# One attention pair loop, three edits: the row-sum scaling goes to ScalarE, the value load to the front of a pair, the value parts of the last pair ahead of its output splits

## The chip, the core and the metric

The kernel runs on one core of one Trainium2 chip. The metric is the device time of one execution in microseconds (us), the median of several runs. TensorE does matmuls, VectorE, ScalarE and GpSimd the elementwise work, SyncE issues most DMA transfers. In the rows the engines are called PE, DVE, ACT, POOL and SP. A difference of under 0.2% can't be told from none for this kernel.

## What is computed

```python
q_bits = (einsum('bhsd,dk->bhsk', q, proj) > 0)          # and k_bits: 6 bits each
mask = q_bucket[:, :, :, None] == k_bucket[:, :, None, :]
scores = where(mask, scale * q @ k.T, -1e9)
attn = exp(scores - max(scores)); attn = attn / (sum(attn) + 1e-9)
x = (attn @ v) reshaped to (B*S, H*D)
x = (sigmoid(x @ w_gate) * (x @ w_val)) @ w_out           # first MLP
out = g(x @ w_in) @ w_out2                                # second MLP, g piecewise
```

There are 2 batches, 8 heads, 768 positions and a head dimension of 64. The MLPs have 1536 rows and a width of 512. 

## The kernel before

The attention takes two heads at a time: eight pairs, numbered 0 to 7 here, of 12 units each (6 blocks of 128 queries for each of two heads). A unit is scored on TensorE (`sc`, line 301), VectorE takes the row maximum (line 309), ScalarE the exponential with the row sums as a by-product (`P` and `st[:, 1]`, line 313). Then TensorE transposes P (`pt`, line 333), ScalarE writes a half-precision high part (line 342) and VectorE the low part (line 345), and TensorE multiplies with the values (`O`, line 384).

Four units share a tile `st` of row sums. Once all four are there, line 316 on VectorE adds 1e-9 and multiplies with the scale of the values, line 319 takes the reciprocal, GpSimd spreads it (`rb`, line 534), TensorE transposes it (`r`, line 516), ScalarE copies it out (`rs`, line 520), and VectorE scales the output with it (`xr`, line 391). That is done three times a pair.

The values of a pair are scaled by a power of two. VectorE takes their largest magnitude (line 353), a DMA lays it out in one row (`vrow<-vm`), VectorE finds the power, and a second DMA brings it back to 128 partitions (`vm<-vrow`, line 362). Then GpSimd makes three things of the values: the scaled `vr` (line 365), the high part `vh` (line 368) and the low part `vl` (line 372).

The order of all this is written out by hand: a table AT gives each step a time in units (a pair is 12 units), `at(...)` collects the steps, and they are issued sorted by it. Each engine then runs its instructions in just that order, and an instruction that waits holds up all behind it on its engine.

In the last pair GpSimd also splits the finished outputs of batch 0 for the MLP that follows (`split_x`, lines 538 and 539: `x_0h`, `x_0l`, and so on). After the attention comes the MLP, which is all TensorE.

Of the kernel before, what the change touches and what calls it, by code (L numbers as in the profile page):

```python
# [7 lines left out]
F32 = mybir.dt.float32  # L8
# [5 lines left out]
AF = mybir.ActivationFunctionType  # L14
ALU = mybir.AluOpType
# [12 lines left out]
def lsh_attention_glu_act(ctx, tc, qt, kt, v, proj, w_gate, w_val, w_out1, w_in2, w_out2, ident_d, code_d, out):  # L28
    nc = tc.nc
# [5 lines left out]
    GI = 2  # L35
# [125 lines left out]
    with ExitStack() as actx:  # L161
        ap = actx.enter_context(tc.tile_pool(name="attn", bufs=2))
        pA = actx.enter_context(tc.tile_pool(name="psA", bufs=2, space=PSUM))
        DMA = nc.gpsimd
        NAT, PR = {}, {}
# [120 lines left out]
        class Unit:  # L286
# [26 lines left out]
                nc.scalar.activation(out=self.P, in_=self.sc[:, :, 0:HN], func=AF.Exp, bias=self.st[:, 0, self.c:self.c + 1], scale=1.0, accum_out=self.st[:, 1, self.c:self.c + 1])  # L313

            def ST1(self):
                nc.vector.tensor_scalar(out=self.st[:, 2], in0=self.st[:, 1], scalar1=1e-9, scalar2=VS[self.b, self.p][1], op0=ALU.add, op1=ALU.mult)

            def ST2(self):
                nc.vector.reciprocal(out=self.st[:, 3], in_=self.st[:, 2])
# [27 lines left out]
        def split_v(b, p, h):  # L347
            vr = VR[b, p]
            if h == 0:
                vm = ap.tile([128, 2], F32, tag="vm", name=f"vm_{b}_{p}")  # L350
                row = ap.tile([1, 260], F32, tag="vrow", name=f"vrow_{b}_{p}")
                VS[b, p] = [row, vm]
                nc.vector.tensor_reduce(out=vm[:, 0:1], in_=vr, op=ALU.max, axis=AX.XY, apply_absolute_value=True)
                nc.sync.dma_start(row[:, 0:128], vm[:, 0:1])
            elif h == 1:
                row, vm = VS[b, p]
                u = row.bitcast(U32)
                nc.vector.tensor_reduce(out=row[:, 128:129], in_=row[:, 0:128], op=ALU.max, axis=AX.X)
                nc.vector.tensor_scalar(out=row[:, 129:130], in0=row[:, 128:129], scalar1=VMIN, scalar2=None, op0=ALU.max)
                nc.vector.tensor_scalar(out=u[:, 130:131], in0=u[:, 129:130], scalar1=0x7F800000, scalar2=None, op0=ALU.bitwise_and)  # L360
                nc.vector.tensor_scalar(out=u[:, 132:260], in0=u[:, 130:131].broadcast_to([1, 128]), scalar1=-1.0, scalar2=268.0 * 2.0 ** 23, op0=ALU.mult, op1=ALU.add)
                nc.sync.dma_start(vm[:, 1:2], row[:, 132:260])
                VS[b, p][1] = vm[:, 1:2]
            elif h == 2:
                nc.gpsimd.tensor_scalar(out=vr, in0=vr, scalar1=VS[b, p][1], scalar2=None, op0=ALU.mult)
            elif h == 3:
                vh = ap.tile([128, 2, NI * D], F16, tag="vh", name=f"vh_{b}_{p}")
                nc.gpsimd.tensor_copy(out=vh, in_=vr)  # L368
                VS[b, p].append(vh)
            else:  # L370
                vl = ap.tile([128, 2, NI * D], F16, tag="vl", name=f"vl_{b}_{p}")
                nc.gpsimd.tensor_tensor(out=vl, in0=vr, in1=VS[b, p][2], op=ALU.subtract)
                VS[b, p].append(vl)
# [13 lines left out]
        def evac(b, p, g, O_ps):  # L387
            cs = slice(g * GN, (g + 1) * GN)
            if g == 0:
                X[b, p] = htile(f"xr_{b}_{p}")  # L390
            nc.vector.scalar_tensor_tensor(out=X[b, p][:, cs], in0=O_ps[:, 0:GN], scalar=1.0 / PSCALE, in1=RS.pop((b, p, g)), op0=ALU.mult, op1=ALU.mult)

        NAT, PR, VR, VS, RS, PT, STS = {}, {}, {}, {}, {}, {}, {}
        NU = B * NP * 2 * NI
        PCS = 3
        un = [Unit(n) for n in range(NU)]
# [1 line left out]
        seq = [(b, p) for b in range(B) for p in range(NP)]  # L398
        UP = 2 * NI

        with tc.manual_schedule():
# [98 lines left out]
            def at(kind, i, q, fn, *args):  # L500
                prog.append((UP * q + (AT[kind][i] if isinstance(kind, str) else kind), len(prog), fn, args))

            PP, NQ = {1: p1}, len(seq)
# [22 lines left out]
                w.O = next(w.pv)  # L526

            def SUM(w):
                w.ST1()
                w.ST2()  # L530

            def RB(w):
# [16 lines left out]
            for q in range(NQ):  # L549
                us = un[UP * q:UP * q + UP]  # L550
                for i, w in enumerate(us):
                    at("QK", i, q, w.QK)
                    at("MAX", i, q, w.MAX)
                    at("EXP", i, q, w.EXP)
                for i in range(PCS * NI):
                    x = fl[NI * q + i // PCS]
                    at("T", i, q, x.T, i % PCS)
                    at("HI", i, q, x.HI, i % PCS)
                    at("LO", i, q, x.LO, i % PCS)
                for i in range(NI // GI):  # L560
                    w = us[2 * GI * i + 2 * GI - 1]
                    at("ST", i, q, SUM, w)
                    at("RB", i, q, RB, w)
                    at("R", i, q, R, w)
                    at("RS", i, q, RSC, w)
                    for s in range(3):
                        at("PV", 3 * i + s, q, PV, w, s)
                    at("EV", i, q, lambda w: evac(*w.O), w)
                b, p = seq[q]
                vs = [AT["VR"][0] - UP, AT["VT"][0] - UP, AT["V2"][0], AT["V3"][0], AT["V4"][0]]  # L570
                if q == 0:
                    vs[:2] = AT["MAX"][1] + 0.001, AT["MAX"][2] + 0.3
                    vs[2] = max(vs[2], vs[1] + 0.5)
                    vs[3] = max(vs[3], vs[2] + 0.1)
                    vs[4] = max(vs[4], vs[3] + 0.1)
                for h, d in enumerate(vs):
                    at(d, 0, q, split_v, b, p, h)
                if q + 1 < NQ:
                    at(5.9, 0, q, load_v, *seq[q + 1])
                    if q:  # L580
                        at(min(AT["SCL"][0], AT["TOP"][0], AT["TOP"][1]) - 0.01, 0, q, prep, q + 1)
                        at("SCL", 0, q, on, q + 1, "scale")
                        for j in range(2):
                            at("TOP", j, q, on, q + 1, "top", j)
                            at("RST", j, q, on, q + 1, "rest", j)
                    for i in range(4):
                        at("Z", i, q, on, q + 1, "z", 3 * i, 3 * i + 3)
                        at("XP", i, q, on, q + 1, "xp", *divmod(i, 2))
                        at("H", i, q, on, q + 1, "H", *divmod(i, 2))
                    at("BITS", 0, q, on, q + 1, "bits")  # L590
                    at(AT["TOP"][0] + 0.001 if q else -0.9, 0, q, on, q + 1, "copy", 0, 0)
                    at(AT["TOP"][1] + 0.001 if q else -0.65, 0, q, on, q + 1, "copy", 1, 0)
                    for j in range(2):
                        for m in range(1, 3):
                            at(AT["Z"][3] + 0.01 * m + 0.001 * j, 0, q, on, q + 1, "copy", j, m)
                        for m in range(3, 5):
                            at(AT["H"][2 * j + 1] + 0.01 * m, 0, q, on, q + 1, "copy", j, m)
                    at(max(AT["H"][3], AT["Z"][3]) + 0.06, 0, q, on, q + 1, "done")
                if q + 2 < NQ:
                    at(0.9, 0, q, load_qk, *seq[q + 2])  # L600
            for i in range(10):
                at(2.0 * i, 0, 1, next, fw, None)
            last = NQ - 1
            for c in range(KC):
                at(5.0 + 1.7 * c, 0, last, split_x, 0, c)
            for c in range(KC - 1):
                at(AT["ST"][2] + 0.1 + 0.01 * c, 0, last, split_x, 1, c)
            at(AT["T"][17] + 0.5, 0, last, gv, 0)
# [173 lines left out]
```

## Time and profile before

| what | value |
|---|---|
| median of 3 runs | 839.19 us (838.26 to 839.45) |
| the profiled execution's own time | 836.99 us |
| its span, first to last instruction | 835.2 us |
| TensorE busy | 808.9 us (97%) |
| VectorE busy | 559.4 us (67%) |
| ScalarE busy | 454.0 us (54%) |
| GpSimd busy | 119.6 us (14%) |

The shares are means over two stages. The attention lies in about the first 265 us, where TensorE, VectorE and ScalarE are all busy most of the time; the MLPs fill the rest. A busy TensorE is not one at its peak, since matmuls overlap and their ends are modelled.

### The profile page before, as it was taken

The numbers are of one execution on the slowest core, as the hardware profiler recorded it, in microseconds if no ns is written. First come the engines' busy times: TensorE is split into PE (matmuls) and PEld (weight loads), VectorE is DVE, ScalarE is ACT, GpSimd is POOL, SyncE is SP. The second block draws the span as 40 slices with busy tenths as digits, with TensorE's granted clock in tenths as the row PEclk, the third lists the DMA queues.
The fourth block names the chain that finished last, engine by engine and source line by source line (L and its number), as shares of the span: only waits on it lengthen the run. The fifth ranks groups of instructions, "written<-read, shape, count | busy, mean of one in ns | idle before, by whom it ended". The sixth has DMA issues, their size and how long they took to land.

```text
span 835.2 us, 13047 instructions
## 1 busy us (share of the span) xinstructions
PE 808.9 (97%) x5098; PEld 738.6 (88%) x5098; DVE 559.4 (67%) x979; ACT 454.0 (54%) x869; POOL 119.6 (14%) x104
## 2 busy tenths in 40 slices
PE   7898999999979999999999999999999999999997
PEld 4787888788758999999999999999989898989896
DVE  5899999999963735434588776999943435343443
ACT  3787887888753423222333445547654545455553
POOL 5525623642174000000000000000000000000000
PEclk8999999999999999999999999999999999999999
DMA  8444434443200521221145330543300001000001
GB/s 229 126 106 110 113 95 118 96 123 67 59 1 1 180 74 51 78 74 51 51 148 188 114 107 1 170 152 118 116 1 1 1 1 75 2 1 1 1 0 77
DMA packets 39709, 64.21 MB, mean 77 GB/s; under 512 B 5316, under 2 KB 28228, under 8 KB 39648
## 3 DMA queue, kind: packets, MB, share of 16 engines
q1 hardware_dynamic: 39168, 63.07, 25.9%
q8 instruction: 40, 0.66, 0.3%
q10 hardware_dynamic: 432, 0.20, 0.1%
q14 instruction: 21, 0.17, 0.1%
q0 software_dynamic: 48, 0.11, 0.0%
HBM read 45.27 MB, written 3.15 MB: 58 GB/s over the span
## 4 chain that ended last, share of the span: by engine, by line
PE 81%; DVE 7%; ACT 6%; DMA 3%; POOL 1%; issue 1%; SPq 0%; ACTq 0%; POOLq 0%; DVEq 0%
PE p L126 5%; PE p L128 5%; PE p L127 5%; PE o L688 5%; PE o L689 5%; PE o L687 5%; PE sc L301 5%; PE pt L333 4%; PE pg L128 4%; PE pg L126 4%; PE pv L126 4%; PE pv L127 4%; PE pv L128 4%; PE pg L127 4%; PE y L127 4%; PE y L126 4%
## 5 line engine op out<-in xcount | busy, mean ns | idle before, releaser
L345 DVE SCALAR_TENSOR_TENSOR PT<-pt,PT 128x512 f16<-128x512 f32 x144 | 95.3, 683 | 19.4 <-ACT PT L342 17.1
L342 ACT ACTIVATE PT<-pt 128x512 f16<-128x512 f32 x144 | 82.2, 597 | 34.9 <-PE pt L333 34.8
L313 ACT ACTIVATE P<-sc,st 128x768 f32<-128x768 f32 x96 | 86.8, 904 | 19.1 <-DVE st L309 18.5
L309 DVE TENSOR_REDUCE st<-sc 128x1 f32<-128x768 f32 x96 | 91.0, 948 | 3.1 <-PE sc L301 2.3
L333 PE MATMUL pt<-ident,P 128*128 128x128 f32 x576 | 80.9, 277 | 5.6 <-DVE PT L345 4.9
L126 PE MATMUL p<-yh,wh_i 128*128 128x384 f32 x256 | 86.0, 336 | 0.1
L128 PE MATMUL p<-yh,wl_i 128*128 128x384 f32 x256 | 86.0, 336 | 0.0
L127 PE MATMUL p<-yl,wh_i 128*128 128x384 f32 x256 | 85.8, 335 | 0.0
L333 PEld LDWEIGHTS pt<-ident,P 128*128 128x128 f32 x576 | 67.3, 141 | 15.2 <-DVE PT L345 9.4
L689 PE MATMUL o<-wh_o,gl 128*128 128x512 f32 x192 | 75.4, 393 | 0.0
L688 PE MATMUL o<-wl_o,gh 128*128 128x512 f32 x192 | 75.3, 392 | 0.0
L687 PE MATMUL o<-wh_o,gh 128*128 128x512 f32 x192 | 74.7, 389 | 0.0
L671 DVE SCALAR_TENSOR_TENSOR g<-p,t 128x384 f32<-128x384 f32 x64 | 35.5, 555 | 48.3 <-ACT t L669 48.3
L154 DVE SCALAR_TENSOR_TENSOR h<-sg,pv 128x384 f32<-128x384 f32 x48 | 26.4, 551 | 50.5 <-PE pv L128 50.5
L150 ACT ACTIVATE sg<-pg 128x384 f32<-128x384 f32 x48 | 23.3, 486 | 63.9 <-PE pg L128 61.9
L384 PE MATMUL O<-PT,vh 128*64 128x256 f16 x576 | 55.3, 279 | 1.9 <-POOL vh L368 1.3
L673 DVE TENSOR_TENSOR gl<-g,gh 128x384 fp32r<-128x384 f32 x64 | 35.7, 557 | 31.5 <-ACT gh L672 31.5
L672 ACT ACTIVATE gh<-g 128x384 fp32r<-128x384 f32 x64 | 33.6, 525 | 42.5 <-DVE g L671 42.3
L668 ACT ACTIVATE t<-p,cst 128x384 f32<-128x384 f32 x64 | 36.7, 573 | 36.8 <-PE p L128 36.8
L126 PEld LDWEIGHTS p<-yh,wh_i 128*128 128x128 f32 x256 | 48.1, 188 | 1.5 <-DVE yl L644 0.4
L127 PEld LDWEIGHTS p<-yl,wh_i 128*128 128x128 f32 x256 | 48.1, 188 | 1.1
L116 DVE TENSOR_TENSOR wl_o<-w_o,wh_o 128x512 fp32r<-128x512 f32 x56 | 38.6, 689 | 15.0 <-ACT wh_o L115 15.0
(264 smaller groups left out, 2032.2 us busy)
## 6 DMA issues: line engine op xcount, KB each, us to landing
wr_o<-in_moe_w_out_dram SPq DMA_DIRECT2D x28, 512.0 KB, 3.5
wr_i<-in_moe_w_in_dram SPq DMA_DIRECT2D x16, 512.0 KB, 3.7
wr_g<-in_moe_w_gate_dram SPq DMA_DIRECT2D x12, 512.0 KB, 3.5
wr_v<-in_moe_w_val_dram SPq DMA_DIRECT2D x12, 512.0 KB, 3.9
n<-in_qt_dram SPq DMA_DIRECT2D x8, 384.0 KB, 3.5
n<-in_kt_dram SPq DMA_DIRECT2D x8, 384.0 KB, 3.8
U<-W SPq DMA_DIRECT2D x16, 192.0 KB, 2.6
vr<-in_v_dram SPq DMA_DIRECT2D x8, 384.0 KB, 3.5
```

The source lines that it names most:

```text
L126: nc.tensor.matmul(ps, lhsT=wh, rhs=rh, start=first, stop=False)
L127: nc.tensor.matmul(ps, lhsT=wh, rhs=rl, start=False, stop=False)
L128: nc.tensor.matmul(ps, lhsT=wl, rhs=rh, start=False, stop=last)
L309: nc.vector.tensor_reduce(out=self.st[:, 0, self.c:self.c + 1], in_=self.sc[:, :, 0:HN], op=ALU.max, axis=AX.XY, negate=True)
L313: nc.scalar.activation(out=self.P, in_=self.sc[:, :, 0:HN], func=AF.Exp, bias=self.st[:, 0, self.c:self.c + 1], scale=1.0, accum_out=self. ...
L333: nc.tensor.transpose(self.ps[m][:, j, :], un[2 * self.n + e].P[:, a, c:c + 128], ident)
L342: nc.scalar.activation(out=self.part(0, m), in_=self.ps[m], func=AF.Copy, scale=PSCALE)
L345: nc.vector.scalar_tensor_tensor(out=self.part(1, m), in0=self.ps[m], scalar=PSCALE, in1=self.part(0, m), op0=ALU.mult, op1=ALU.subtract)
L384: nc.tensor.matmul(O_ps[r, 0:GN], lhsT=vv[m][:, e, i * D:(i + 1) * D], rhs=PT[:, l, e * NI + i, :], start=(s == 0), stop=(s == len(steps) ...
L687: nc.tensor.matmul(oacc[i], lhsT=gh[:, ts], rhs=wh, start=(fc == 0), stop=False)
L688: nc.tensor.matmul(oacc[i], lhsT=gh[:, ts], rhs=wl, start=False, stop=False)
L689: nc.tensor.matmul(oacc[i], lhsT=gl[:, ts], rhs=wh, start=False, stop=(fc == F2 - 1))
```

## The change

Line 316 leaves VectorE. In its place ScalarE does `sum * scale + 1e-9 * scale` in one activation, issued right behind the fourth exponential of a group; the product `1e-9 * scale` is made once a pair by a further activation of one element per partition. The reciprocal stays on VectorE where it was. The load of the next pair's values is issued at time 0.8 of a pair instead of 5.9. In the last pair the three value parts are issued on GpSimd from time 1.5 on (6.89 before), and the output splits from 2.2 on, 1.5 apart (from 5.0 on, 1.7 apart).

```diff
             def ST1(self):
-                nc.vector.tensor_scalar(out=self.st[:, 2], in0=self.st[:, 1], scalar1=1e-9, scalar2=VS[self.b, self.p][1], op0=ALU.add, op1=ALU.mult)
+                vm = VM[self.b, self.p]
+                if self.i // GI == 0:
+                    nc.scalar.activation(out=vm[:, 2:3], in_=vm[:, 1:2], func=AF.Copy, scale=1e-9)
+                nc.scalar.activation(out=self.st[:, 2], in_=self.st[:, 1], func=AF.Identity, scale=vm[:, 1:2], bias=vm[:, 2:3])
...
-                vm = ap.tile([128, 2], F32, tag="vm", name=f"vm_{b}_{p}")
+                vm = VM[b, p] = ap.tile([128, 3], F32, tag="vm", name=f"vm_{b}_{p}")
...
             def SUM(w):
-                w.ST1()
                 w.ST2()
...
                     w = us[2 * GI * i + 2 * GI - 1]
+                    at(max(AT["EXP"][4 * i:4 * i + 4]) + 0.001, 0, q, w.ST1)
                     at("ST", i, q, SUM, w)
...
+                elif q == NQ - 1:
+                    vs[2:] = (max(vs[1] + 0.5, 1.5) + 0.1 * i for i in range(3))
                 for h, d in enumerate(vs):
                     at(d, 0, q, split_v, b, p, h)
                 if q + 1 < NQ:
-                    at(5.9, 0, q, load_v, *seq[q + 1])
+                    at(0.8, 0, q, load_v, *seq[q + 1])
...
             for c in range(KC):
-                at(5.0 + 1.7 * c, 0, last, split_x, 0, c)
+                at(2.2 + 1.5 * c, 0, last, split_x, 0, c)
```

TensorE's order is the same before and after. The other engines' orders change at these places (the numbers at the ends of names are buffer numbers, which differ between the two programs).

VectorE, pair 4, second group of four units, before:

```order
L309 TENSOR_REDUCE st_0_0_2_2003<-sc_0_1_3_2090 128x1
L345 SCALAR_TENSOR_TENSOR PT_0_1_2079<-pt_1_2095,PT_0_1_2079 128x4x128
L345 SCALAR_TENSOR_TENSOR PT_0_0_1967<-pt_2_2102,PT_0_0_1967 128x4x128
L316 TENSOR_SCALAR st_0_0_2_2003<-st_0_0_2_2003,vm_0_1791 128x4
L319 RECIPROCAL st_0_0_2_2003<-st_0_0_2_2003 128x4
L309 TENSOR_REDUCE st_0_0_4_2170<-sc_0_0_4_2126 128x1
```

The same place in the change:

```order
L309 TENSOR_REDUCE st_0_0_2_2011<-sc_0_1_3_2097 128x1
L348 SCALAR_TENSOR_TENSOR PT_0_1_2087<-pt_1_2102,PT_0_1_2087 128x4x128
L348 SCALAR_TENSOR_TENSOR PT_0_0_1973<-pt_2_2109,PT_0_0_1973 128x4x128
L322 RECIPROCAL st_0_0_2_2011<-st_0_0_2_2011 128x4
L309 TENSOR_REDUCE st_0_0_4_2175<-sc_0_0_4_2133 128x1
```

The row of line 316 is gone; the reciprocal, line 322 now, stands where it stood.

ScalarE at the same place, before:

```order
L313 ACTIVATE P_0_0_3_2083,st_0_0_2_2003<-sc_0_0_3_2042,st_0_0_2_2003 128x768
L238 ACTIVATE H_1_1_1776<-xp_1_1_1_2086,cst 128x384
L342 ACTIVATE PT_0_1_2079<-pt_1_2095 128x4x128
L342 ACTIVATE PT_0_0_1967<-pt_2_2102 128x4x128
L313 ACTIVATE P_0_1_3_2146,st_0_0_2_2003<-sc_0_1_3_2090,st_0_0_2_2003 128x768
L240 ACTIVATE H_1_1_1780<-xp_1_1_0_2122,cst 128x384
```

and in the change:

```order
L313 ACTIVATE P_0_0_3_2090,st_0_0_2_2011<-sc_0_0_3_2050,st_0_0_2_2011 128x768
L238 ACTIVATE H_1_1_1780<-xp_1_1_1_2093,cst 128x384
L345 ACTIVATE PT_0_1_2087<-pt_1_2102 128x4x128
L345 ACTIVATE PT_0_0_1973<-pt_2_2109 128x4x128
L313 ACTIVATE P_0_1_3_2151,st_0_0_2_2011<-sc_0_1_3_2097,st_0_0_2_2011 128x768
L319 ACTIVATE st_0_0_2_2011<-st_0_0_2_2011,vm_0_1795 128x4
L240 ACTIVATE H_1_1_1784<-xp_1_1_0_2129,cst 128x384
```

The new activation (line 319 of the changed file) stands between the fourth exponential and the operand `H` of the next pair.

GpSimd from the end of pair 6 through the last pair (`vr_3`, `vh_3`, `vl_3` are the last pair's value parts, `rb_2_1_5` the third reciprocal of pair 6, `rb_3_1_1` and `rb_3_1_3` the first two of pair 7), before:

```order
L534 COPY rb_2_1_5_3260<-st_2_0_4_3044 128x256
L534 COPY rb_3_1_1_3359<-st_3_0_0_3164 128x256
L538 CAST x_0h<-xr_0_519 128x768
L539 TENSOR_TENSOR x_0l<-xr_0_519,x_0h 128x768
L538 CAST x_1h<-xr_1_972 128x768
L539 TENSOR_TENSOR x_1l<-xr_1_972,x_1h 128x768
L365 TENSOR_SCALAR vr_3_3005<-vr_3_3005,vm_3_3093 128x768
L368 CAST vh_3_3413<-vr_3_3005 128x768
L538 CAST x_2h<-xr_2_1417 128x768
L539 TENSOR_TENSOR x_2l<-xr_2_1417,x_2h 128x768
L372 TENSOR_TENSOR vl_3_3457<-vr_3_3005,vh_3_3413 128x768
L534 COPY rb_3_1_3_3487<-st_3_0_2_3287 128x256
```

and in the change:

```order
L368 TENSOR_SCALAR vr_3_2832<-vr_3_2832,vm_3_3100 128x768
L371 CAST vh_3_3265<-vr_3_2832 128x768
L375 TENSOR_TENSOR vl_3_3269<-vr_3_2832,vh_3_3265 128x768
L536 COPY rb_2_1_5_3272<-st_2_0_4_3051 128x256
L540 CAST x_0h<-xr_0_520 128x768
L541 TENSOR_TENSOR x_0l<-xr_0_520,x_0h 128x768
L540 CAST x_1h<-xr_1_974 128x768
L541 TENSOR_TENSOR x_1l<-xr_1_974,x_1h 128x768
L536 COPY rb_3_1_1_3380<-st_3_0_0_3171 128x256
L540 CAST x_2h<-xr_2_1420 128x768
L541 TENSOR_TENSOR x_2l<-xr_2_1420,x_2h 128x768
L540 CAST x_3h<-xr_3_1860 128x768
```

The value parts moved ahead of the output splits, and also ahead of `rb_2_1_5`; the first two output splits moved ahead of `rb_3_1_1`, the other two ahead of `rb_3_1_3`.

SyncE, pair 2, the load of pair 3's values (`vr_3`), before:

```order
L362 DMA vm_2_904<-vrow_2_905 128x1x1
L171 DMA n_1_0_1065<-in_qt_dram 128x768
L171 DMA n_1_0_1067<-in_kt_dram 128x768
L279 DMA U_0_3_887<-W_0_3_888 64x768
L279 DMA U_0_3_891<-W_0_3_892 64x768
L279 DMA W_0_3_888<-N_0_3_890 64x768
L279 DMA W_0_3_892<-N_0_3_894 64x768
L279 DMA N_0_3_890<-H_0_3_889 64x768
L279 DMA H_0_3_889<-U_0_3_887 64x768
L177 DMA vr_3_1252<-in_v_dram 128x2x384
L279 DMA N_0_3_894<-H_0_3_893 64x768
```

and in the change:

```order
L365 DMA vm_2_906<-vrow_2_907 128x1x1
L177 DMA vr_3_1067<-in_v_dram 128x2x384
L171 DMA n_1_0_1070<-in_qt_dram 128x768
L171 DMA n_1_0_1072<-in_kt_dram 128x768
L279 DMA U_0_3_889<-W_0_3_890 64x768
L279 DMA U_0_3_893<-W_0_3_894 64x768
L279 DMA W_0_3_890<-N_0_3_892 64x768
L279 DMA W_0_3_894<-N_0_3_896 64x768
L279 DMA N_0_3_892<-H_0_3_891 64x768
L279 DMA H_0_3_891<-U_0_3_889 64x768
L279 DMA N_0_3_896<-H_0_3_895 64x768
```

The load moved from behind two copies of the next pair's operands to a place right behind the scale's return, ahead of the loads of `n`.

## Rows read from the trace of the kernel before

**Rows 1.** windows of all engines: busy us (instructions), granted clock, DMA share, GB/s.

```profile
108.00:156.00 48.00, 47.01 (x410) 39.64 (x409) 44.49 (x73) 39.97 (x84) 20.55 (x17) 1.00 0.44 111
...
298.00:346.00 48.00, 48.00 (x279) 48.00 (x278) 21.16 (x41) 11.88 (x22) 0.00 (x0) 1.00 0.22 67
```

**Rows 2.** chain that ended last, items of the sum's scaling: start, us, what.

```profile
33.56 1.70 DVE st L316
...
64.28 0.94 DVE st L316
...
152.40 1.63 DVE st L316
```

**Rows 3.** the same chain, narrower window, where it leaves and rejoins TensorE.

```profile
151.37 1.00 ACT P L313 x2
...
158.07 0.97 PE sc L301 x4
```

**Rows 4.** all instructions of VectorE's line 316 and of line 319, durations in ns.

```profile
L316 DVE TENSOR_SCALAR st<-st,vm x24: 206/221/1684, 29.5 to 259.2; 128x4 f32<-128x4 f32 x24
...
L319 DVE RECIPROCAL st<-st x24: 177/178/179, 29.8 to 259.5; 128x4 f32<-128x4 f32 x24
```

**Rows 5.** timeline of pair 4, GpSimd and ScalarE: start, duration, instruction, [idle before].

```profile
152.35 1.64 POOL L372 TENSOR_TENSOR vl<-vr,vh 128x768 f16<-128x768 f32 x1
...
155.18 0.90 ACT L313 ACTIVATE P<-sc,st 128x768 f32<-128x768 f32 x1 [1.29 <-DVE st L309]
```

**Rows 6.** chain, two TensorE pieces at full pace.

```profile
134.72 0.78 PE O L384 x12
...
135.49 0.90 PE sc L301 x4
```

**Rows 7.** timeline of GpSimd in the last pair.

```profile
227.78 0.40 POOL L534 COPY rb<-st 128x256 f32<-128x256 f32 x1 [14.80 <-DVE st L319]
...
241.02 2.20 POOL L365 TENSOR_SCALAR vr<-vr,vm 128x768 f32<-128x768 f32 x1
243.28 0.82 POOL L368 CAST vh<-vr 128x768 f16<-128x768 f32 x1
...
246.72 1.64 POOL L372 TENSOR_TENSOR vl<-vr,vh 128x768 f16<-128x768 f32 x1
```

**Rows 8.** timeline of TensorE in the last pair.

```profile
228.37 0.41 PE L516 MATMUL r<-ident,rb 128*128 128x128 f32 x2 [0.51 <-DVE PT L345]
...
244.16 0.30 PE L384 MATMUL O<-PT,vh 128*64 128x256 f16 x2 [1.34 <-POOL vh L368]
...
248.41 0.43 PE L384 MATMUL O<-PT,vl 128*64 128x256 f16 x2 [3.95 <-POOL vl L372]
...
251.06 1.25 PE L333 MATMUL pt<-ident,P 128*128 128x128 f32 x8
```

**Rows 9.** SyncE's timeline, and DMA issues with us to landing, last pair.

```profile
224.40 0.52 SPq L362 DMA_DIRECT2D vm<-vrow  x1
...
vm<-vrow SPq DMA_DIRECT2D x1, 0.5 KB, 2.0
```

**Rows 10.** window just behind the last pair's stall, columns as in group 1.

```profile
248.40:251.10 2.70, 2.69 (x15) 2.12 (x16) 0.00 (x0) 0.00 (x0) 2.62 (x3) 0.50 0.00 0
```

**Rows 11.** groups of ScalarE by shape: count, busy us, mean ns, idle before.

```profile
L520 ACT ACTIVATE rs<-r 128x256 f32<-128x256 f32 x23 | 8.9, 385 | 1.1 <-PE r L516 0.3
...
L342 ACT ACTIVATE PT<-pt 128x512 f16<-128x512 f32 x144 | 82.2, 597 | 34.9 <-PE pt L333 34.8
...
L240 ACT ACTIVATE H<-xp,cst 128x384 fp32r<-128x384 f32 x14 | 8.2, 588 | 0.0
```

**Rows 12.** timeline of VectorE in pair 2.

```profile
99.91 0.95 DVE L353 TENSOR_REDUCE vm<-vr 128x1 f32<-128x768 f32 x1 [0.62 <-DMA vr<-in_v_dram]
```

**Rows 13.** timelines of SyncE and ScalarE in pair 0.

```profile
23.19 0.55 SPq L362 DMA_DIRECT2D vm<-vrow  x1
...
25.06 1.12 ACT L342 ACTIVATE PT<-pt 128x512 f16<-128x512 f32 x2
```

## What was predicted before the run

> **What bounds the kernel now.** Read the windows first [rows 1]. Between 108 and 156 us TensorE is busy 47.0 of 48 us, VectorE 44.5, ScalarE 40.0; between 298 and 346 us TensorE is busy all the time and nothing else matters. So whatever the change does lies in the attention, and there three engines run almost level: a microsecond taken from VectorE is worth one only where TensorE has room to take it up. The later stage follows whenever the attention ends, so what is won or lost in it goes into the whole time unchanged.
>
> Then the chain of work that ended last. In a pair it runs over TensorE for most of the time and leaves it once, from 151.37 us (an exponential) to 158.07 us (scores that wait for one) [rows 3]. In that stretch lies line 316, the step that is moved, with 1.63 us [rows 2]. The chain holds line 316 six times, in pairs 0 (1.70), 1 (0.94) and 3 to 6 (1.63 or 1.64 each) [rows 2].
>
> Then the line itself: its 24 instructions have a median of 221 ns and a maximum of 1684 [rows 4]. The timeline tells why: in pair 4 GpSimd's `vl` starts at 152.35 us and takes 1.64, to 153.99 [rows 5]; line 316 starts at 152.40 on the chain and is held 1.63, to 154.03 [rows 2]. It is held as long as GpSimd's instruction runs. The reciprocal behind it takes 177 to 179 ns in all 24 cases [rows 4], so it doesn't share that wait. ScalarE stands idle for 1.29 us behind it, waiting for VectorE's maximum [rows 5].
>
> Last, the last pair. TensorE waits 1.34 us for `vh` and, one pair of matmuls later, 3.95 us for `vl` [rows 8]; GpSimd makes them at 243.28 and 246.72 us, behind output splits [rows 7].
>
> **The change, part by part.**
>
> *The price on ScalarE.* No row shows an activation of 128x4 with two operands per partition. The shapes without such an operand give 385 ns for 256 elements and 597 for 512 [rows 11], so 0.83 ns an element and 173 ns fixed. With one such operand 384 elements take 588 [rows 11], against 173 + 318 = 491: about 97 ns an operand. An estimate is then 173 + 194 + 3 = 0.37 us for the new step and 0.17 for the one-element product: 24 and 8 of them, 10.2 us in all. The bounds are nothing, where ScalarE waits for TensorE anyway (34.9 us before line 342 [rows 11]), and 10.2 us if all of it is on the path.
>
> *Pairs 3 to 6.* The reciprocal no longer waits for GpSimd but for ScalarE. The fourth exponential and its read of the sums end at 152.37 us [rows 3], the new step at about 152.77, the reciprocal at 152.95, so the next maximum starts some 1.2 us earlier than at about 154.1, where 152.40 + 1.63 and most of a reciprocal put it. ScalarE's next exponential can follow by 1.29 - 0.37 = 0.92 [rows 5], as the new step uses up part of its idle time. TensorE has 1.0 us of visible room in 48 [rows 1] and some more inside its overlaps. I take 0.8 a pair, near ScalarE's 0.92: **3.2 us**, with bounds of 0 (TensorE keeps its pace) and 4 x 1.2 = 4.8.
>
> *Pairs 0 and 1.* Here VectorE has the weights of the MLP as well, and a gain passes on: in pair 1 the 0.94 of [rows 2], of which I take 0.9. In pair 0 1.70 goes, say 0.9 of it felt; but there the step also adds a wait. The first new activation needs `vm`, which is issued at 23.19 us [rows 13] and lands 2.0 us later if it behaves like the last one [rows 9], at 25.2, while ScalarE wants to go on at 25.06 [rows 13]. Behind it stand the high parts of line 342 and the next exponential, and VectorE and TensorE wait for those. Landing, product and step cost 0.14 + 0.17 + 0.37, about 0.7, and more if the value load, now ahead of it on SyncE's queue, holds the transfer up. I put pair 0 at 0, between a loss of 1 and a gain of 1: **0.9 us** for both pairs.
>
> *The value load.* It only cost something once: in pair 2 VectorE waited 0.62 us for it [rows 12]. The new place is a pair's length ahead of the reduction. Its bytes now run with the next but one pair's operands, whose use is most of a pair away. I take **0.4 us**, between 0 and 0.62.
>
> *The other ScalarE steps.* Sixteen of the 24 steps, and the products, fall where line 316 was not on the chain. VectorE is relieved of 0.22 each [rows 4], which TensorE can't use there, and ScalarE gets 0.37. I take a **loss of 0.6 us**, between 0 and the 7.3 that 16 x 0.37 + 8 x 0.17 add up to.
>
> *The last pair.* From where it began to wait, 244.16 - 1.34 = 242.82, to the transpositions at 251.06 TensorE took 8.24 us [rows 8] for twelve value matmuls and one set of scores, which take 0.78 + 0.90 = 1.68 elsewhere [rows 6]. So the stall costs 6.56 us; part is that the clock was granted at 0.50, 1.2 GHz, from 248.4 us on [rows 10], when TensorE had done almost nothing since 242.8. All of this goes, as the value parts come 15 us earlier.
>
> But something else is late then. GpSimd now does the value parts ahead of `rb_2_1_5`. They can start when `vm` is back: 224.40 + 2.0 = 226.4 us [rows 9]. They take 2.20 + 0.82 + 1.64 and `rb` 0.40 [rows 7], so `rb` is ready at about 231.5 instead of 228.2. TensorE's `r` started at 228.37 [rows 8] and would wait until 231.6: a **new stall of 3.3 us**, 3.2 to 3.5 with the gaps between GpSimd's instructions. Queued behind `r` are the next scores, and ScalarE's copy `rs` stands ahead of an exponential, so all three engines stop, and little of it can be hidden. TensorE's clock stood at 1.2 GHz behind the two waits of 1.34 and 3.95 us [rows 8, 10]; what it does after one of 3.3 no row says. At 1.2 GHz for as long as before (2.7 us [rows 10], half of the work lost) the price is about 1.3 us; I take 0.5, between 0 and 1.3, as the new wait is the shorter. The output splits come early enough: those moved ahead of `rb_3_1_1` and `rb_3_1_3` end before these are due. Net: 6.56 - 3.3 - 0.5 = **2.7 us**, between 1.8 and 3.3.
>
> **The sum.** 3.2 + 0.9 + 0.4 - 0.6 + 2.7 = 6.6 us. The profiled execution has a span of 835.2 us and a time of 836.99; it would become 828.6 and 830.4. The median of the runs is 839.19, 2.2 above the profiled one; the prediction is for the median: **832.6 us**, 0.8% faster.
>
> **Where the skill speaks to this.** The rows show that line 316 is held by a GpSimd instruction and that the reciprocal, with one SBUF operand, never was [rows 4, 5]. The Trainium skill, "SBUF — State Buffer", section "Who interferes with whom", says that the two engines share a pair of ports under an exclusive lock for a whole instruction, and lists copy, cast and tensor_scalar as takers, not the reciprocal. The trace agrees on tensor_scalar with 1.63 us against 0.22. By the rule the reciprocal stays free, and the sum stands.
>
> ScalarE's step costs 0.37 us by rows where VectorE's costs 0.22 undisturbed [rows 4, 11]. The Trainium skill, "ScalarE: Activation LUTs", section "Rules for kernel authors", advises VectorE for additions and multiplications. No run here shows the step on ScalarE. By the rule the move would be a loss, which is the second rival below.
>
> **The rivals.**
>
> 1. *TensorE keeps its pace.* In pairs 3 to 6 it is busy 98% [rows 1], and what VectorE wins is lost in waits elsewhere. Against it speaks that the chain leaves TensorE there. The 3.2 falls away: 839.2 - 3.4 = 835.8 us.
> 2. *ScalarE becomes the bound; slower.* Of the 10.2 us of new work at lines 318 and 319 all end up on the path. Before the loss on ScalarE the sum is 7.2, so the change turns slower once over 70% of the 10.2 are felt; at all of it the time is 839.2 - 7.2 + 10.2 = 842.2. For it speaks that ScalarE is busy 83% [rows 1] and serves both others; against it that it waits so much for TensorE [rows 11].
> 3. *The wait moves to the reciprocal.* It now stands where line 316 was, beside `vl`, and is held as long. Then pairs 0, 1 and 3 to 6 win nothing: 0.4 - 0.6 + 2.7 = 2.5, 836.7 us. Against it: 24 times 178 ns.
> 4. *More than that.* The pairs win all that VectorE wins (4.8, and 1.9 in pairs 0 and 1), the clock holds, ScalarE hides its steps: 4.8 + 1.9 + 0.6 + 3.3 = 10.6, 828.6 us.
>
> **How the numbers follow.** I give the forecast 0.50, rival 1 0.17, rival 2 0.08, rival 3 0.07 and rival 4 0.18. The forecast's own range is 830.5 to 834.5, from the bounds of its terms taken by halves. A range from 828.0 to 836.8 takes in rival 1, most of 3 and most of 4, and leaves out rival 2 and the tails, about 2 in 10. A measurement can tell 0.2% or 1.7 us from no change, so below 837.5 is faster: the forecast, rivals 1 and 4 and half of rival 3, 0.89. Within 0.2% 0.05 is left, from rivals 2 and 3, and slower 0.06 from rival 2.
>
> **What the profile will show.** Line 316 gone from VectorE and 24 activations of 0.3 to 0.4 us on ScalarE; the exponential behind the second group with hardly any idle time before it, and the period of pairs 3 to 6 shorter by 0.8 us; the reciprocal at 178 ns still. In the last pair no wait for `vh` or `vl`, but one of some 3.3 us of TensorE's `r` for `rb`, with the clock at full or half behind it. In pair 0 ScalarE waits briefly for `vm`. The prediction is wrong if `r` waits much longer than that, if the reciprocal is held, or if the period of a pair does not shrink.

## The result, and the profile after

| | before | after |
|---|---|---|
| median of 4 runs | 838.95 us (838.26 to 839.45) | 829.59 us (828.2 to 832.19) |
| ratio of the times | | 0.9893, 95% interval 0.9866 to 0.9919 |
| the profiled execution | 836.99 us, span 835.2 | 832.19 us, span 830.4 |
| VectorE busy | 559.4 us | 547.7 us |
| ScalarE busy | 454.0 us | 461.4 us |

The change makes the kernel 1.1% faster. A second measurement gave 829.76 us against 838.39, ratio 0.9899 (0.9883 to 0.9914), with a second trace. The first trace is of the longest of its four executions, which matters below.

First the moved step itself, all its instructions in the changed kernel (line 319 is the step on ScalarE, 322 the reciprocal on VectorE; both groups come from the view of one line):

```profile
L319 ACT ACTIVATE st<-st,vm x24: 388/389/391, 25.7 to 248.5; 128x4 f32<-128x4 f32 x24
...
  DVE st L322: 3.0, 6
...
L322 DVE RECIPROCAL st<-st x24: 154/167/179, 30.4 to 252.6; 128x4 f32<-128x4 f32 x24
```

This answers to [rows 4]: no instruction is held any more. The reciprocal is never held by GpSimd, but six times it waits 0.5 us for ScalarE. In pair 4 it looks like this on the timelines of ScalarE, of VectorE and of GpSimd:

```profile
150.69 0.39 ACT L319 ACTIVATE st<-st,vm 128x4 f32<-128x4 f32 x1
150.98 0.56 ACT L240 ACTIVATE H<-xp,cst 128x384 fp32r<-128x384 f32 x1
...
152.19 0.91 ACT L313 ACTIVATE P<-sc,st 128x768 f32<-128x768 f32 x1
```

```profile
151.11 0.18 DVE L322 RECIPROCAL st<-st 128x4 f32<-128x4 f32 x1 [0.51 <-ACT st L319]
151.20 0.94 DVE L309 TENSOR_REDUCE st<-sc 128x1 f32<-128x768 f32 x1
```

```profile
150.42 1.66 POOL L375 TENSOR_TENSOR vl<-vr,vh 128x768 f16<-128x768 f32 x1
```

So the reciprocal starts in the middle of `vl` and still takes 0.18 us. The trace of before shows much less of that: behind a line 316 that was held, the reciprocal came only after the end of `vl`, as here in pair 4, where `vl` ended at 153.99 us [rows 5]:

```profile
154.06 0.18 DVE L319 RECIPROCAL st<-st 128x4 f32<-128x4 f32 x1
```

The step lasts 0.39 us but the next activation starts 0.29 us after it: activations overlap a little. The exponential behind it, ahead of which ScalarE stood idle for 1.29 us before [rows 5], follows at once. The windows, same stretch as [rows 1]:

```profile
108.00:156.00 48.00, 47.77 (x419) 40.80 (x418) 42.67 (x70) 43.07 (x94) 22.18 (x20) 1.00 0.45 120
```

TensorE gained 0.8 us of busy time. VectorE went from 44.5 to 42.7 and ScalarE from 40.0 to 43.1: they have changed places.

In the last pair the waits for `vh` and `vl` [rows 8] are gone, and the predicted new one is there. TensorE's and GpSimd's timelines:

```profile
222.21 0.52 PE L301 MATMUL sc<-W,W 128*128 128x384 f32 x2
226.64 0.69 PE L519 MATMUL r<-ident,rb 128*128 128x128 f32 x2 [3.90 <-POOL rb L536]
226.98 0.99 PE L301 MATMUL sc<-H,H 128*128 128x384 f32 x2
```

```profile
221.42 2.21 POOL L368 TENSOR_SCALAR vr<-vr,vm 128x768 f32<-128x768 f32 x1 [13.24 <-PE pt L336]
223.70 0.82 POOL L371 CAST vh<-vr 128x768 f16<-128x768 f32 x1
224.61 1.64 POOL L375 TENSOR_TENSOR vl<-vr,vh 128x768 f16<-128x768 f32 x1
226.19 0.40 POOL L536 COPY rb<-st 128x256 f32<-128x256 f32 x1
```

The value parts come ahead of `rb_2_1_5`, and TensorE's `r` waits for it. Around it the granted clock (the figure right behind the five engines' busy times) falls to half, 1.2 GHz; a value between 0.50 and 1.00 is the mean of a stretch with both:

```profile
222.00:226.00 4.00, 0.74 (x5) 0.40 (x3) 2.41 (x5) 1.54 (x4) 3.85 (x3) 0.83 0.00 0
226.00:230.00 4.00, 3.36 (x15) 3.27 (x15) 0.96 (x1) 2.25 (x6) 3.92 (x5) 0.50 0.00 0
230.00:232.00 2.00, 2.00 (x12) 1.74 (x12) 1.72 (x3) 1.57 (x4) 1.85 (x2) 0.63 0.00 0
232.00:236.00 4.00, 4.00 (x41) 3.40 (x41) 3.84 (x7) 3.36 (x7) 1.08 (x2) 1.00 0.00 0
```

**Where the time came from.** TensorE's instructions stand in the same order in these kernels, so each matmul can be found in two traces, and its start in the trace of before, less its start in the other, is a lead. The table gives it for E1 to E8, E10 and E11 below ("again" is the second trace of the changed kernel). It is worked out from the traces and is not a view of the profile.

```
start in before    after  again    E1     E2     E6     E3     E5     E7     E4     E8    E10    E11
 24.25 z           -0.28  -0.35  -0.50   1.57  -0.75   1.49  -0.88   0.36  -0.55   1.24  -0.02  -0.35
 34.73 sc          -1.38  -2.00  -2.13  -0.38  -1.71  -0.30  -0.89  -2.38  -2.01  -1.28  -1.17  -1.76
 39.92 sc           0.37  -0.25  -0.37  -0.39   0.02  -0.32  -0.76  -0.64  -0.26   0.47   0.55  -0.17
 57.81 pt           0.34  -0.30  -1.88  -0.38   0.00  -0.34  -0.79  -0.83  -0.27   0.45   0.57  -0.22
104.57 pt           0.98   0.39  -1.20  -0.23   0.66  -0.49  -0.73  -1.03   0.38   1.10   0.87   0.21
223.06 sc           5.56   4.98   1.66  -0.15   5.25  -0.48  -0.58  -0.48   4.91   5.67   6.41   4.59
228.37 r            1.73   1.15   1.49  -0.15   5.08  -3.83  -3.98  -4.38   4.74   5.50   6.52   0.92
233.63 pt           0.08   0.12   0.93  -0.13   4.53  -4.89  -5.15  -5.42   4.17   4.94   6.42  -0.09
253.68 r            7.00   7.04   0.34  -0.79   3.58   2.03   1.77   1.45  11.09  11.86  13.34   6.84
261.33 pv (MLP)     6.55   6.61  -0.09  -0.80   3.15   2.01   1.74   0.58  10.66  11.44  13.30   6.41
521.86 y            6.44   6.70  -0.10  -0.75   3.02   2.03   1.52   0.55  10.56  11.41  13.23   6.31
828.61 o (end)      4.36   6.62  -0.17  -2.00   2.69   1.06   1.19   0.51  10.25  11.86  13.68   6.84
```

Pairs 3 to 6 lie between the rows at 105 and 223 us. There the changed kernel wins 4.6 us; then it loses 5.5 at the new stall and wins 6.9 where the old one was. Two reservations: the trace of before lies 2 us under its own median, so most leads are 1 to 2.3 us below the gains of the medians (E7's only 0.1, since its traced execution is the fastest of its eleven, 1.6 us under their median). And the first trace lost another 2.1 us between 546 and 607 us, in the MLP; the second trace of the same kernel lost 0.1 there, so that belongs to one execution and not to the change.

### The profile page after: what moved, and what is told of

Read it like the earlier page. It is cut to its first block, busy times and chain, and to the rows that moved or that the text cites. A ratio compares the mean times of both kernels' runs of the same rounds, so it can differ in the third digit from the quotient of the medians.

```text
span 830.4 us, 13004 instructions
## 1 busy us (share of the span) xinstructions
PE 808.0 (97%) x5098; PEld 739.1 (89%) x5098; DVE 547.7 (66%) x955; ACT 461.4 (56%) x901; POOL 120.0 (14%) x104
## 4 chain that ended last, share of the span: by engine, by line
PE 83%; DVE 5%; ACT 5%; DMA 4%; issue 1%; POOL 0%; SPq 0%; DVEq 0%; ACTq 0%; POOLq 0%
PE sc L301 6%; PE pt L336 5%; PE o L694 5%; PE o L693 5%; PE o L692 5%; PE p L126 5%; PE p L128 5%; PE p L127 5%; PE O L387 5%; PE pg L128 4%; PE pv L128 4%; PE pg L126 4%; PE pv L127 4%; PE pv L126 4%; PE pg L127 4%; PE y L126 3%
## 5 line engine op out<-in xcount | busy, mean ns | idle before, releaser
L677 ACT ACTIVATE gh<-g 128x384 fp32r<-128x384 f32 x64 | 33.6, 525 | 42.7 <-DVE g L676 42.6
```

## The experiments

In each, the theory of the prediction (its terms) stands against at least one other. Times are medians; "won" is against the kernel before, run beside it (838.25 to 838.61 us).

### E1, E2, E3, E6: the edits by themselves

E1 takes from the change only the step on ScalarE, E2 only the value load, E3 only the last pair's order, E6 the first two:

```diff
# E2, in the kernel before
-                    at(5.9, 0, q, load_v, *seq[q + 1])
+                    at(0.8, 0, q, load_v, *seq[q + 1])
# E3, in the kernel before
+                elif q == NQ - 1:
+                    vs[2:] = (max(vs[1] + 0.5, 1.5) + 0.1 * i for i in range(3))
...
-                at(5.0 + 1.7 * c, 0, last, split_x, 0, c)
+                at(2.2 + 1.5 * c, 0, last, split_x, 0, c)
```

> The first edit alone: the step on ScalarE behind the exponential, value load and last pair as before. By the prediction's terms (3.2 for pairs 3 to 6, 0.9 for pairs 0 and 1, less 0.6 for ScalarE) 838.95 - 3.5 = 835.4 us. If the pairs keep all that VectorE wins (4 x 1.15 in pairs 3 to 6, 0.85 in pair 1) and ScalarE hides its steps: 833.5 us. If TensorE keeps its pace: 838 us or more.

> The second edit alone: the load of the next pair's values at 0.8 of a pair instead of 5.9. By the prediction 0.4 us won, 838.5; VectorE's wait of 0.62 us for the values in pair 2 gone. Rival: the wait was hidden anyway, 838.9; or the load in front of the vm transfer of pair 0 delays it, and the kernel loses some tenths there.

> The third edit alone: in the last pair the value parts ahead of rb_2_1_5 and the output splits earlier. By the prediction's terms 6.56 - 3.3 - 0.5 = 2.7 us won, 836.2 us. By the trace of the changed kernel, where the new stall of r with the half clock behind it cost TensorE 5.05 us, 6.56 - 5.05 = 1.5, 837.4 us. If the old wait for vh and vl was worth less than its 6.56: no gain, 838.9 or more.

> The first and the second edit together, the last pair as before. Each alone won 1.8 and 0.3 us. By those sizes, which simply add: 836.5 us. If the load is what held the first edit back (VectorE waits 3.9 us in five places for the values with the first edit alone, and never in the changed kernel), the two together win 5 to 6 us: about 833 us, no wait of the maximum of the values.

Measured: E1 836.82 us, won 1.8 (ratio 0.9978, 0.9967 to 0.9989). E2 838.29, won 0.3 (0.9992, 0.9983 to 1.0). E3 836.03, won 2.6 (0.9968, 0.9956 to 0.998). E6 833.49, won 4.8 (0.9939, 0.9926 to 0.9951). E2's gain can't be told from none, but VectorE's wait of 0.62 us is gone in its trace. The three single edits add up to 4.7 us, the change wins 8.6 to 9.4: about half of it lies in their being together.

Why E1 falls short is in VectorE's waits of E1 (us in total, times, longest):

```profile
DVE vm L356 <- DMA vr<-in_v_dram: 3.9, 5, 1.7
```

Before the change there was one such wait of 0.62 us [rows 12], and in the changed kernel and E6 there is none. E1's SyncE and VectorE in pair 0:

```profile
36.06 0.46 SPq L279 DMA_DIRECT2D H<-U  x1
36.57 0.58 SPq L177 DMA_DIRECT2D vr<-in_v_dram  x1
```

```profile
41.15 0.95 DVE L356 TENSOR_REDUCE vm<-vr 128x1 f32<-128x768 f32 x1 [1.70 <-DMA vr<-in_v_dram]
```

The load stands in SyncE's queue behind a copy `H<-U`, which waits 2.1 us for the landing of the copy `N<-H` ahead of it, and the values arrive 4.6 us after the load is issued. With VectorE quicker, its reduction is there first and waits. The lead shows the 1.5 us lost between 39.9 and 57.8 us, and in pairs 3 to 6 E1 gains 2.9 where E6 gains 4.6. So behind the first edit the second is worth 3.3 us by the medians (836.82 to 833.49, with about 1.4 either way by the two intervals), where alone it is next to nothing.

### E4: the value parts behind `rb_2_1_5`

```diff
-                    vs[2:] = (max(vs[1] + 0.5, 1.5) + 0.1 * i for i in range(3))
+                    vs[2:] = (max(vs[1] + 0.5, 1.83) + 0.1 * i for i in range(3))
```

> The changed kernel with the three value parts of the last pair issued right behind rb_2_1_5 instead of right ahead of it, everything else as changed. If the new stall of r and the half clock behind it are lost time, they go: 829.6 - 5.0 = 824.6 us, no wait of r over 1 us, clock at 1.00 there. Rival: only the wait itself comes back, 829.6 - 3.9 = 825.7. Rival: the value parts, some 5 us later, make the matmuls with the values wait, or rb_3_1_1 is late, and the time stays near 829.

Measured: 826.62 us, won 12.0 (ratio 0.9852, 0.9838 to 0.9867), 3.0 less than the changed kernel, whose second interval (0.9883 to 0.9914) lies clear above. GpSimd, and the windows where the clock was at half:

```profile
223.04 0.40 POOL L536 COPY rb<-st 128x256 f32<-128x256 f32 x1 [14.22 <-DVE st L322]
223.43 2.20 POOL L368 TENSOR_SCALAR vr<-vr,vm 128x768 f32<-128x768 f32 x1
```

```profile
222.00:226.00 4.00, 3.74 (x24) 2.96 (x24) 3.94 (x6) 3.70 (x10) 2.89 (x3) 1.00 0.00 0
226.00:230.00 4.00, 3.41 (x30) 2.69 (x29) 3.44 (x6) 3.47 (x8) 3.83 (x4) 1.00 0.00 0
```

No wait of `r` for `rb` is left, the clock stays at 2.4 GHz, and TensorE waits nowhere for the value parts, which come 2 us later. So the stall and the clock behind it were lost time: 4.1 us by the leads at the MLP's start (10.66 against 6.55 and 6.61), 3.0 by the medians. The expected 5.0 left out that TensorE loses 0.7 us at this place without the stall too (E4, 4.91 to 4.17).

### E5: the step on VectorE in another form

The load and the last pair are as in the changed kernel, but the step is back on VectorE in its old place. Its line, against that of the kernel before:

```diff
-                nc.vector.tensor_scalar(out=self.st[:, 2], in0=self.st[:, 1], scalar1=1e-9, scalar2=VS[self.b, self.p][1], op0=ALU.add, op1=ALU.mult)
+                nc.vector.scalar_tensor_tensor(out=self.st[:, 2], in0=self.st[:, 1], scalar=1e-9, in1=VM[self.b, self.p][:, 1:2].broadcast_to([128, SG]), op0=ALU.add, op1=ALU.mult)
```

> The changed kernel with the step back on VectorE in its old place, but as one scalar_tensor_tensor, whose second operand is a tile, in place of tensor_scalar; no new work on ScalarE. If the long hold belongs to the form tensor_scalar: 24 instructions of about 0.2 us, none over 0.4, and a time of 828 to 830 us like the changed kernel's. If any small VectorE instruction on these operands is held beside GpSimd's vl, and only the move to ScalarE avoids it: a maximum of 1.6 us again, the 4 to 5 us of the pairs lost, 834 us.

Measured: 835.36 us, won 2.9 (ratio 0.996, 0.9946 to 0.9974), which is what E3 wins: of the first two edits' gain nothing is left. The line, and GpSimd and VectorE in pair 3:

```profile
L316 DVE SCALAR_TENSOR_TENSOR st<-st,vm x24: 140/152/1574, 30.3 to 257.4; 128x4 f32<-128x4 f32 x24
```

```profile
123.92 1.65 POOL L372 TENSOR_TENSOR vl<-vr,vh 128x768 f16<-128x768 f32 x1
```

```profile
124.03 1.55 DVE L316 SCALAR_TENSOR_TENSOR st<-st,vm 128x4 f32<-128x4 f32 x1
125.62 0.18 DVE L319 RECIPROCAL st<-st 128x4 f32<-128x4 f32 x1
```

The step is quicker undisturbed (152 ns against 221), yet is held just as before, until GpSimd's `vl` ends at 125.57 us (123.92 + 1.65); the reciprocal then comes behind the end of `vl`. So the hold doesn't belong to tensor_scalar alone, and the theory that this other form would do has fallen. Others were not tried. In the lead, pairs 3 to 6 gain 0.15 us. The Trainium skill, "SBUF — State Buffer", section "Who interferes with whom", says that a VectorE instruction with two inputs in SBUF contends with a GpSimd instruction that reads SBUF, and that one with at most one such input doesn't, outside the modes that use both ports. By that rule E5's step is held and the reciprocal is free; E5's trace agrees for the step, with 1574 ns against 152, and the changed kernel's for the reciprocal, with 178 ns inside `vl`.

### E8: pair 0's first step later

On top of E4, ScalarE's first product and step stand ahead of the high part before the reciprocal, and not right behind the fourth exponential:

```diff
-                    at(max(AT["EXP"][4 * i:4 * i + 4]) + 0.001, 0, q, w.ST1)
+                    at(max(AT["EXP"][4 * i:4 * i + 4]) + 0.001 if q or i else AT["HI"][3] - 0.01, 0, q, w.ST1)
```

> The kernel with the value parts behind rb_2_1_5 (826.6 us), and in pair 0 the first product and step later on ScalarE, just ahead of the high part before the reciprocal, when vm has long been back. If the 0.65 us that TensorE falls behind at 28 us come from ScalarE's wait for vm and the two activations behind it: 826.0 us. Rival: what is won there was given back anyway by 38 us, 826.6.

Measured: 824.99 us (824.67 to 828.47), ratio 0.9851 (0.9833 to 0.9869), where E4 has 0.9852. The median is 1.6 lower, the ratio the same, so the times don't settle it. The leads give a hint: 0.47 against -0.26 at 39.9 us, and that 0.7 stays to 223 us. But E8's execution was 1.8 us ahead of E4's at 24 us, so one trace of each doesn't prove it.

### E7, E10, E11: what a step costs on ScalarE and on VectorE

E7 makes the step on ScalarE twice; E11 makes the reciprocal twice on VectorE. E10, on top of E8, has no such step at all; it leaves out the 1e-9 and puts the scale into VectorE's output scaling (cut here: the lines that take out the step itself, and that make `k`, a view of the row that carries the scale):

```diff
# E7
                 nc.scalar.activation(out=self.st[:, 2], in_=self.st[:, 1], func=AF.Identity, scale=vm[:, 1:2], bias=vm[:, 2:3])
+                nc.scalar.activation(out=self.st[:, 2], in_=self.st[:, 1], func=AF.Identity, scale=vm[:, 1:2], bias=vm[:, 2:3])
# E11
                 nc.vector.reciprocal(out=self.st[:, 3], in_=self.st[:, 2])
+                nc.vector.reciprocal(out=self.st[:, 3], in_=self.st[:, 2])
# E10
-                nc.vector.reciprocal(out=self.st[:, 3], in_=self.st[:, 2])
+                nc.vector.reciprocal(out=self.st[:, 3], in_=self.st[:, 1])
...
+                nc.vector.tensor_scalar(out=k[:, :, 1], in0=u[:, 130:131].broadcast_to([1, 128]), scalar1=(-12.0 - 14.0) * 2.0 ** 23, scalar2=None, op0=ALU.add)
-                nc.sync.dma_start(vm[:, 1:2], row[:, 132:260])
+                nc.sync.dma_start(vm[:, 1:3], row[:, 132:388])
...
-            nc.vector.scalar_tensor_tensor(out=X[b, p][:, cs], in0=O_ps[:, 0:GN], scalar=1.0 / PSCALE, in1=RS.pop((b, p, g)), op0=ALU.mult, op1=ALU.mult)
+            nc.vector.scalar_tensor_tensor(out=X[b, p][:, cs], in0=O_ps[:, 0:GN], scalar=VM[b, p][:, 2:3], in1=RS.pop((b, p, g)), op0=ALU.mult, op1=ALU.mult)
```

> The changed kernel with the new step on ScalarE made twice, 24 activations of 0.39 us more, the same numbers written again. If ScalarE hides most of it, as the prediction's loss of 0.6 us for all the steps supposes: at most 1 us more, 830.6. If ScalarE is the bound, so that the new work is felt in full: 24 x 0.30 to 0.39, 7 to 9 us more, 837 to 839 us.

> The kernel of the last experiment (825.0 us) without the step on any engine: the reciprocal is taken of the sums themselves, and the inverse of the scale, a power of two, is made once a pair beside the scale and multiplied in where the output is scaled already. It leaves out the 1e-9, which a sum of at least 1 doesn't feel in 32 bits. If ScalarE pays for each step in full, as the doubling says (8.0 us for 24 more): 24 x 0.3, 7 us less, 818 us. If the first set of steps lay hidden, as the prediction's 0.6 us supposes: 824 us or more.

> The changed kernel with the reciprocal made twice, 24 VectorE instructions of 0.17 us more. If VectorE's undisturbed 0.22 us per step were worth nothing, as the prediction had it for 16 of 24 steps: at most 0.5 us more, 830.1. If VectorE is felt in full as ScalarE is: 24 x 0.17, 4 us more, 833.6.

Measured: E7 837.61 us (ratio 0.9988, 0.9979 to 0.9996), 8.0 more than the changed kernel. E11 830.66 us (0.9912, 0.9899 to 0.9925), 1.0 more, though its interval overlaps that of the changed kernel. E10 823.75 us (0.9831, 0.9818 to 0.9845), 1.2 less than E8, with intervals that overlap; by the leads 1.8 less. E10 has the lowest median of this study, 1.7% under the kernel before.

So a second set of steps costs 8 us, and taking out the first set gives back at most 2. E7's ScalarE in pair 4, and who waits for its second step:

```profile
154.48 0.39 ACT L319 ACTIVATE st<-st,vm 128x4 f32<-128x4 f32 x1
154.90 0.39 ACT L320 ACTIVATE st<-st,vm 128x4 f32<-128x4 f32 x1
155.20 0.56 ACT L240 ACTIVATE H<-xp,cst 128x384 fp32r<-128x384 f32 x1
```

```profile
  DVE st L323: 5.6, 6
```

The second step takes 0.42 us of ScalarE's queue: it writes what the first wrote, and starts only behind its end. 24 times that is 10 us, of which 5.9 show in the leads (6.44 against 0.55 at 521 us) and 8.0 in the medians. The reciprocal waits for ScalarE 5.6 us in the same six places, where it was 3.0. So E7 does two things, it fills ScalarE and it sends VectorE on later; the second comes to 2.6 us in all by these waits, less than half of what the leads lose. VectorE in E11, in contrast, hides at least three quarters of its 24 x 0.17 us. That ScalarE's slack was one step and no more fits these numbers, but no run here varies the dose more finely, so it stays argued. E10 pays something in its turn: VectorE's output scaling reads its factor per partition there and takes a median of 475 ns, against 415 in E8:

```profile
L394 DVE SCALAR_TENSOR_TENSOR xr<-O,rs x24: 408/415/425, 43.1 to 255.9; 128x256 f32<-128x256 f32 x24
```

```profile
L390 DVE SCALAR_TENSOR_TENSOR xr<-O,vm,rs x24: 469/475/484, 43.1 to 254.1; 128x256 f32<-128x256 f32 x24
```

That is 1.4 us more on VectorE, so what E10 wins is a net.

### The changed kernel again

> The changed kernel once more, for a second trace of it. Time 829.6 us; the 2.1 us that TensorE lost in the MLP between 546 and 607 us of the first trace smaller or gone, if they belong to the one execution and not to the change; the wait of r for rb 3.9 us again.

Measured: 829.76 us; its MLP loses 0.1 us where the first trace lost 2.1, and TensorE's wait is back:

```profile
PE r L519 <- POOL rb L536: 3.9, 1, 3.9
```

In pair 0 this execution waited for `vm` much longer than the first (0.14 us there, from 25.36 to 25.50). The transfer took 3.2 us to land, against 2.0 in the first trace; why, no run here shows:

```profile
26.13 0.20 ACT L318 ACTIVATE vm<-vm 128x1 f32<-128x1 f32 x1 [1.05 <-DMA vm<-vrow]
```

## Why the prediction was right, and which of its terms were not

The direction, the mechanism and the places were as predicted. The time, 829.59 us, came out 3.0 us below the forecast of 832.6: inside the wide range of 828.0 to 836.8, but below the forecast's own of 830.5 to 834.5. By its own steps:

- **What holds line 316, and that the reciprocal is free: right.** The reciprocal takes 154 to 179 ns, so rival 3 fell; E5 shows that the hold comes back when a step with two operands stands there on VectorE again. The ground given for the second half was thin: in the trace of before the reciprocal stood behind the end of `vl` wherever line 316 was held, and started beside `vl` only once (95.38 us, pair 2), so its 24 times 178 ns said little of what happens there.
- **The price on ScalarE: right.** 0.389 us for 0.37, 0.19 for 0.17. In the queue a step takes only 0.29.
- **Pairs 3 to 6, 0.8 us each, 3.2: mis-sized.** They win 4.6 (0.98 to 5.56), 1.15 a pair. That is VectorE's whole 1.2, not ScalarE's 0.92: TensorE took all of it up, and rival 1 fell. But E1 wins only 2.9 there; the rest needs the load.
- **The value load, 0.4: right alone, but not a term by itself.** "It only cost something once" was read from the old schedule, as if the load kept its distance when VectorE got quicker. Alone it won 0.3, but behind the first edit 3.3: without it the quicker pairs waited for their values in five of eight cases (E1). For all three edits together the sum is not wrong by this, since the terms of the pairs took it for granted that the values are there; for E1 it is, whose 835.4 came out as 836.82.
- **Pairs 0 and 1, 0.9 with pair 0 at nothing: about right.** From 24 to 105 us, with pair 2 and its wait for the values, the changed kernel gains 1.3 in the first trace and 0.7 in the second. Pair 0 by itself (24 to 40 us) gives 0.65 and 0.1; ScalarE's wait for `vm` was 0.14 and 1.05 us there.
- **The other ScalarE steps, a loss of 0.6: not contradicted.** No run takes away these sixteen alone; taking all 24 away wins 1.2 to 1.8 us net (E10). But E7, with the reservation made there, speaks for ScalarE having hardly room for more, so rival 2, with 8 in 100, was nearer than the prediction saw. "TensorE can't use" VectorE's 0.22 elsewhere is about borne out: 4.1 us more on VectorE cost 1.0 at most (E11). The Trainium skill, "ScalarE: Activation LUTs", section "Rules for kernel authors", advises VectorE for additions and multiplications; by that rule the move would lose. E1, which won 1.8 us by the move alone, doesn't agree, here where the VectorE form is held for 1.6 us.
- **The last pair, 2.7: the stalls right in kind, both larger than said.** The old stall was worth 6.9 us (0.08 to 7.00 in the lead) for 6.56; the new one put `r` back by 3.8 (5.56 to 1.73) for 3.3. Over the matmuls behind it, at half clock, another 1.65 went in the first trace (1.73 to 0.08) and 1.0 in the second. E4 loses 0.6 over the same matmuls at full clock (4.74 to 4.17), so the clock's own price lies between 0.5 and 1.65, and the 0.5 taken was its low end. From 223 to 254 us the net is 1.4 to 2.1; E3 alone has 2.5, and won 2.6 by the medians. In the changed kernel the edit is worth more by the medians, 3.7 to 3.9 (833.49 to 829.76 or 829.59). E6, with the old order, loses 1.7 us against the trace of before from 223 to 254 us (5.25 to 3.58). Of these, 0.7 are gone by 234 us, as in E4, 0.3 come back in between, and 1.2 go behind the old stall (4.79 at 251 us to 3.58). There the two traces differ in the clock. Here are the windows behind the stall, of the kernel before first, then of E6; the matmuls with `vl` start at 248.41 us in the one and at 243.62 in the other:

```profile
248.00:252.00 4.00, 3.59 (x21) 3.02 (x22) 0.00 (x0) 0.09 (x1) 3.92 (x5) 0.57 0.00 0
252.00:256.00 4.00, 3.53 (x45) 2.76 (x45) 2.55 (x5) 3.73 (x9) 3.84 (x4) 1.00 0.00 0
```

```profile
244.00:248.00 4.00, 4.00 (x22) 3.25 (x18) 0.00 (x1) 0.63 (x2) 3.84 (x4) 0.50 0.00 0
248.00:252.00 4.00, 3.52 (x35) 2.67 (x34) 2.58 (x4) 2.73 (x7) 3.92 (x4) 0.84 0.00 0
```

E1 and E2, which keep the old order too, lose 0.9 and 0.7 at the same place. So the trace of before had the mildest half clock of these four, each a single execution, and a net read against it comes out low.

The sum was 6.6 us, and the second trace's lead is 6.6 at the end. That agreement is luck, from errors that cancel: by the leads the pairs came out above their terms, the last pair below. Rival 4's time, 828.6, is nearer to the medians (its sum counts the 0.6 as a gain and leaves out the load's 0.4; put right it is 10.4, for 828.8). Its main part, that the pairs win all that VectorE wins, is what happened; its other part, that the clock holds, is not. And the forecast was made from the trace of before, 2.2 us under the median of its runs; the medians won 8.6 to 9.4. Where the other executions of the kernel before spend those 2 us, no trace here shows. The clock behind the old stall may be a part of it: the traced execution has a mean granted clock of 0.994, and of the 47 that ran beside the experiments only two have that, at 837.52 and 836.53 us, while the others, at 0.988 to 0.993, have a median of 838.4. It stays open how much of the 2 us that is.

## What to carry to other kernels

A transfer that is just early enough is priced against the new schedule, not the old one: where an edit speeds up a loop, recompute which waits come due next, and test edits in pairs, since here the parts won 4.7 us alone and about 9 together. When something is moved ahead on an in-order queue, look at the small instruction that it passes: putting the 0.4 us `rb` back in front of 4.7 us of value parts won 3 us more (E4). And "the engine has room" needs a dose: taking out the first set of 24 small steps on ScalarE won under 2 us net, adding a second cost 8. Last, one trace of a kernel is one execution: look whether its time and its mean clock are those of the others before you size a term by it.

## What the runs showed of the hardware that was not expected

- The clock behind one and the same 3.9 us stall differs between executions of the same kernel. In the second trace it fell to 1.2 GHz later than in the first, whose windows stand above (0.83, 0.50, 0.63):

```profile
222.00:226.00 4.00, 1.31 (x9) 0.98 (x8) 2.99 (x5) 2.07 (x4) 3.83 (x3) 1.00 0.00 0
226.00:230.00 4.00, 2.78 (x15) 2.63 (x15) 0.96 (x1) 2.27 (x6) 3.92 (x5) 0.75 0.00 0
230.00:232.00 2.00, 2.00 (x12) 1.74 (x12) 1.74 (x3) 1.54 (x4) 1.92 (x2) 0.65 0.00 0
```

- A VectorE step of 152 ns with two operands in SBUF was held for up to 1574 ns beside GpSimd's `vl` (E5); a reciprocal, with one, took 178 ns in the middle of `vl` (the changed kernel).
- Reading its factor per partition instead of as a constant made a VectorE operation of 256 elements per partition 60 ns longer (415 to 475, E8 and E10).
